# Attention with relative bias, then a bilinear feed-forward: fewer warm-up matmuls, another order around pairs 0, 1, 3 and 4, value products moved by one unit, and a last output tile stored in two halves

## The chip, the cores and the metric

The kernel runs on one core of a Trainium2 chip. The metric is the device time of one execution in microseconds (us). For the kernel before, the median of 11 runs is 427.14 us (425.99 to 428.47).

## The reference

The inputs are q, k and v in float32, each of 8 batches, 8 heads, 576 positions and 64 columns, a table of 32 bias buckets for 8 heads, and three weights: two of 512 x 1536 and one of 1536 x 512.

```python
scores = scale * np.matmul(q, k.transpose(0, 1, 3, 2))      # scale = 1/8
bias = bias_table[bucket]                                   # bucket depends on |i - j| alone
scores = scores + bias.transpose(2, 0, 1)[None, :, :, :]
attn = np.exp(scores - np.max(scores, axis=-1, keepdims=True))
attn = attn / (np.sum(attn, axis=-1, keepdims=True) + 1e-09)
x = np.matmul(attn, v).transpose(0, 2, 1, 3).reshape(8 * 576, 512)
out = ((x @ w_a) * (x @ w_b)) @ w_out                       # 4608 x 512, float32
```

## The kernel before, in words

**Pairs and steps.** The 64 combinations of batch and head are worked in 32 pairs of two heads; pair p belongs to batch p // 4. The 576 positions are four blocks of 128 and a tail of 64; the tails of the two heads share one block. For each pair TensorE (PE) makes the scores transposed, with keys on the partitions: `qk1(p, t)` (L334) for key block t, two matmuls of 64 x 512, one for each head, into one PSUM tile called `sc` of which there are two. `qk_tail(p)` (L361) makes the scores of the tails in a third use of the same two tiles and in a small extra bank. ScalarE (ACT) takes the exponential of each: `ex(p, t)` (L347) over 128 x 1024, `ex_tail(p)` (L374). VectorE (DVE) multiplies the band near the diagonal by exponentials of the bias: `mul` (L353) and `mul_tail` (L381), with tables `W` and `Wt` that a small matmul, an exponential and a trip through DRAM make at the start. `av(p, jq)` (L389) is the value product of query block jq, nine matmuls of 65 or 130 columns; blocks 0 to 2 go to one PSUM bank, 3 and 4 to another tile. A column of ones in the values gives the sums, and `norm(p, 0)` and `norm(p, 3)` (L441) divide by them on DVE and write `XG`. `t_x` (L456) transposes `XG` into the input `xn` of the feed-forward, either on PE (and then `c_x` copies it from PSUM) or, for the pairs in the set `XD` (L450), by DMA from the SP queue.

**q and k.** Both must be transposed before the scores. For pairs 0, 1 and 3 float32 inputs are transposed on PE (L559, L579, L588), for the other pairs of the first three batches bfloat16 inputs by `t_q` and `t_k` (L286, L306) with copies `c_q` and `c_k`; `tails_next` (L593) does the tails of the first pairs. From batch 3 on DMA transposes do this ("turns").

**The feed-forward.** Eight chunks of 512 positions, one for each batch, and a ninth chunk with all the tails. A chunk is 36 units of four matmuls of 128 x 128 x 512 each: 24 units `ff_a` and `ff_b` (L512, L518) for twelve slices of the hidden width, then four output tiles of three units, `ff_o` (L522). `ff_a` ends with a copy `ha` on ACT, `ff_b` with a product `g` on DVE, the third unit of an output tile with a copy `ob` on ACT and a store on the SP queue. The last chunk's stores are two for each tile, of 64 rows.

**PSUM.** Eight banks: four for the two `sc` tiles, one called AV, one called TR (transposes, and value products 3 and 4 of the early pairs), two called FF. From step 12 on (`R3`, L110) the units take turns on the two FF banks and TR, and value products 3 and 4 use AV, as do products 0 to 2.

**Order.** The order on each engine is that of the code. Pairs 0 to 2 are a loop (L601), pair 3 and the start of pair 4 are written out (L644 to L695), and from step 4 on a list of steps (L714 to L757) has places for units, marked U. A table of quotas says how many units a step puts there: 12, 7, 6, 4 and 4 in steps 4 to 8, nine in each later one. In step s pair s gets its scores and pair s-1 its value products. All loads of v, k, q and the weights but the first are issued by GpSimd (POOL) in one queue.

## Time and profile before

| | |
|---|---|
| median of 11 runs | 427.14 us (425.99 to 428.47) |
| profiled execution | 426.22 us |
| span from the first to the last instruction in it | 424.5 us |
| PE | busy 408.2 us, 96% of the span |
| ACT | busy 243.0 us, 57% |
| DVE | busy 199.0 us, 47% |
| POOL | busy 119.4 us, 28% |
| units' matmuls (lines L508 and L527) | 110.6, 109.6 and 99.5 us of PE's busy time |
| data moved | 40.31 MB |

The profiled execution takes 1.7 us more than its span, and lies 0.92 us under the median of the runs. A row of the time-ordered view gives the start, the duration, the engine, the line, what is written from what, and the count of merged instructions; in brackets stands how long the engine was idle before it and what ended that. A matmul's duration includes the time until its last result is out, so two neighbours overlap: of four matmuls of 512 columns in a row only the starts tell the pace. A few matmul records are missing. Some lines of the views name a releaser whose semaphore was in use again later, so the name is not always that of the true cause.

### The profile page before, as it was taken

How to read it: one execution, taken by the hardware profiler on the slowest of the kernel's cores; microseconds unless marked ns; L12 is line 12 of the kernel's file. 1: busy time of each engine (PE TensorE's matmuls, PEld its weight loads, DVE VectorE, ACT ScalarE, POOL GpSimd, SP SyncE). 2: the span in 40 equal slices, each digit the busy share in tenths (PEclk: the TensorE clock that was granted, in tenths of full speed). 3: DMA queues.
4: the chain of work that ended last, by engine and by line, in shares of the span. 5: the costliest groups of instructions: out<-in, count | busy, mean ns of one | idle time of the engine just before them, and what ended most of it. 6: DMA issues, size and time to landing. Idle time of an engine off the chain costs nothing.

```text
span 424.5 us, 8421 instructions
## 1 busy us (share of the span) xinstructions
PE 408.2 (96%) x3355; PEld 204.0 (48%) x3410; DVE 199.0 (47%) x492; ACT 243.0 (57%) x343; POOL 119.4 (28%) x161
## 2 busy tenths in 40 slices
PE   8798899999999999999999999999999999999995
PEld 3474455555544444444444444444444454444442
DVE  3684576556552555245535553355425550331420
ACT  3986476666665666676656665666656642322321
POOL 9998829603527000920073003000000000000000
PEclk9999999999999999999999999999999999999999
DMA  9999999993919950999099917931020012002004
GB/s 157 191 172 174 159 173 142 176 174 33 105 20 158 180 72 15 143 183 117 15 87 197 141 20 50 173 74 34 15 88 32 10 17 99 2 0 100 1 4 96
DMA packets 162855, 40.31 MB, mean 95 GB/s; under 512 B 153368, under 2 KB 158016, under 8 KB 162816
## 3 DMA queue, kind: packets, MB, share of 16 engines
q0 software_dynamic: 110448, 18.75, 60.4%
q1 hardware_dynamic: 51248, 20.72, 25.4%
q8 instruction: 26, 0.43, 0.4%
q10 hardware_dynamic: 1120, 0.30, 0.3%
q14 instruction: 13, 0.11, 0.1%
HBM read 38.77 MB, written 9.45 MB: 114 GB/s over the span
## 4 chain that ended last, share of the span: by engine, by line
PE 88%; POOL 4%; DMA 4%; issue 1%; DVE 1%; ACT 0%; POOLq 0%; DVEq 0%
PE pa L508 22%; PE pb L508 22%; PE po L527 22%; PE av L409 8%; PE qk L339 7%; PE av L400 3%; DMA vm<-in_v_dram 2%; DMA qtl<-in_q_dram 2%; PE qkt L364 2%; PE qkt L367 1%; DMA vt<-in_v_dram 1%; POOL vm L123 1%; PE trx L472 1%; POOL W L166 1%; PE trk L311 0%
## 5 line engine op out<-in xcount | busy, mean ns | idle before, releaser
L350 ACT ACTIVATE at<-qk 128x1024 bf16<-128x1024 f32 x128 | 126.0, 1024 | 21.9 <-PE qk L339 21.9
L520 DVE TENSOR_TENSOR g<-pb,ha 128x512 bf16<-128x512 f32 x108 | 74.7, 692 | 116.7 <-PE pb L508 95.1
L508 PE MATMUL pa<-xn,wa 128*128 128x512 bf16 x421 | 110.6, 379 | 2.3 <-ACT ha L515 1.6
L508 PE MATMUL pb<-xn,wb 128*128 128x512 bf16 x414 | 109.6, 379 | 0.8
L515 ACT ACTIVATE ha<-pa 128x512 f32<-128x512 f32 x108 | 64.6, 598 | 70.8 <-PE pa L508 69.3
L527 PE MATMUL po<-wo,g 128*128 128x512 bf16 x410 | 99.5, 379 | 1.2
L358 DVE TENSOR_TENSOR at<-at,W 128x512 bf16<-128x512 bf16 (+1 forms) x128 | 60.0, 483 | 9.8 <-ACT at L350 8.2
L508 PEld LDWEIGHTS <-wa 128*128 128x128 bf16 x432 | 38.9, 98 | 49.5 <-issue 10.3
L531 ACT ACTIVATE ob<-po 128x512 f32<-128x512 f32 x36 | 21.5, 597 | 69.9 <-PE po L527 67.9
L508 PEld LDWEIGHTS <-wb 128*128 128x128 bf16 x432 | 39.2, 98 | 45.5 <-issue 5.4
L527 PEld LDWEIGHTS <-g 128*128 128x128 bf16 x432 | 38.4, 98 | 45.4 <-issue 7.4
L123 POOL DMA_DIRECT2D vm<-in_v_dram x32 | 28.1, 906 | 106.6 <-PE av L409 105.4
L409 PE MATMUL av<-vm,at 128*128 128x65 bf16 x992 | 43.3, 193 | 0.0
L409 PEld LDWEIGHTS <-at 128*128 128x128 bf16 x992 | 39.5, 97 | 3.9
L445 DVE RECIPROCAL rc<-av 128x6 f32<-128x6 f32 x64 | 12.0, 188 | 57.2 <-PE av L409 55.4
L400 PE MATMUL av<-vt,att 128*128 128x130 bf16 x156 | 34.9, 224 | 0.4
L378 ACT ACTIVATE att<-qkt 128x1024 bf16<-128x1024 f32 x32 | 32.6, 1020 | 0.0
L446 DVE TENSOR_TENSOR XG<-av,rc 128x384 bf16<-128x384 f32 x64 | 31.4, 491 | 2.2
L123 POOL DMA_DIRECT2D qn<-in_q_dram x28 | 24.4, 926 | 26.7 <-PE trq L291 19.2
L123 POOL DMA_DIRECT2D kn<-in_k_dram x28 | 24.5, 920 | 5.6 <-DMA vm<-in_v_dram 2.5
L339 PE MATMUL qk<-QTb,KTb 64*128 64x512 bf16 x160 | 24.2, 381 | 0.0
L400 PEld LDWEIGHTS <-att 128*128 128x128 bf16 x156 | 15.3, 98 | 15.3 <-DVE XG L446 10.7
(114 smaller groups left out, 239.6 us busy)
## 6 DMA issues: line engine op xcount, KB each, us to landing
out_dram<-ob SPq DMA_DIRECT2D x32, 256.0 KB, 4.5
vm<-in_v_dram POOLq DMA_DIRECT2D x28, 128.0 KB, 5.2
qn<-in_q_dram POOLq DMA_DIRECT2D x24, 128.0 KB, 7.7
kn<-in_k_dram POOLq DMA_DIRECT2D x24, 128.0 KB, 8.9
wa<-in_moe_w_a_dram POOLq DMA_DIRECT2D x3, 512.0 KB, 7.0
wb<-in_moe_w_b_dram POOLq DMA_DIRECT2D x3, 512.0 KB, 8.8
wo<-in_moe_w_out_dram POOLq DMA_DIRECT2D x1, 1536.0 KB, 13.4
out_dram<-ob SPq DMA_DIRECT2D x8, 128.0 KB, 2.4
```

The source lines that it names most:

```text
L123: nc.gpsimd.dma_start(out=(vm[b % 2][:, h0:h1, t, 0:Dh] if dst is None else dst[b % 2][:, :].rearrange("p (t h d) -> p t h d", h=H, t=NM)[ ...
L339: nc.tensor.matmul(out=ps[:, hh, :], lhsT=kT_(p, t)[r, :], rhs=qT[r, :, :], start=True, stop=True)
L350: nc.scalar.activation(out=at[:, :, :], in_=ps[:, :, :], func=ACTF.Exp, scale=scale)
L358: nc.vector.tensor_tensor(out=at[:, :, lo:hi], in0=at[:, :, lo:hi], in1=w[:, :, y:(None if z < 0 else z):-1], op=MULT)
L378: nc.scalar.activation(out=at[:, 0:1024].rearrange("p (a x) -> p a x", a=2), in_=ps[:, :, :], func=ACTF.Exp, scale=scale)
L400: nc.tensor.matmul(out=pav[:, slot, :, :], lhsT=x, rhs=vt[b // 2 % 2][:, 4 * i + hp, :, 0:Dh + 1], start=fresh, stop=True, skip_group_chec ...
L409: nc.tensor.matmul(out=pav[:, slot, hh, :], lhsT=x, rhs=vm[i][:, 2 * hp + hh, t, 0:Dh + 1], start=False, stop=True, skip_group_check=True)
L446: nc.vector.tensor_tensor(out=xg[:, j0:j0 + n, :, :], in0=pav[:, 0:n, :, 0:Dh], in1=rc.unsqueeze(3).to_broadcast([128, n, 2, Dh]), op=MULT)
L508: nc.tensor.matmul(out=ff[key][:, :], lhsT=w[df // FW][:, mc, 128 * (df % FW):128 * (df % FW) + 128], rhs=xn_sb[mc][:, xin(c)], start=(i = ...
L515: nc.scalar.activation(out=ha[:, :], in_=ff["pa"][:, :], func=ACTF.Copy)
L520: nc.vector.tensor_tensor(out=g_sb[df][:, :], in0=ff["pb"][:, :], in1=ff["ha"][:, :], op=MULT)
L527: nc.tensor.matmul(out=po[:, :], lhsT=g_sb[df][:, 128 * tt:128 * tt + 128], rhs=wo_sb[:, df, :], start=(df == 0), stop=(df == NDF - 1))
```

## The change

It has six parts.

1. Five warm-up matmuls on zeros ahead of the first transposes become three. Two such matmuls are put elsewhere: one ahead of the second and one ahead of the third score block of pair 0 (`fill`).
2. The first turn of the loop over pairs 0 to 2 is written out. In it the first score block of pair 1 and its exponential stand ahead of the tail scores of pair 0, and the multiplications `mul(0, 0)` to `mul(0, 2)` behind them.
3. At pair 3 the copy `c_x(2)` goes from DVE to ACT, the transposes `t_k(4)` stand behind the value products of pair 3, and all scores of pair 4 move behind the first units, into step 4, whose list now has a unit at each of twelve places and ends with two of them.
4. In steps 5 to 10 `t_k(s + 1)` stands one place for a unit later, behind `mul(s, 2)`.
5. From step 12 on, value products 3 and 4, `norm(s-1, 3)` and the DMA transposes behind them come one unit later. The set `XD` begins at pair 8 instead of pair 11, so that pairs 8, 9 and 10 are transposed by DMA.
6. The last output tile of the last chunk is made in two halves of 256 columns, in two PSUM banks. The first half is copied on ACT, the second on DVE, and of each half 64 rows are stored from the SP queue and 64 from ACT's.

The change moves instructions. On ACT, at pairs 0 and 1 (`at0_3` is pair 0's fourth exponential, `att0` takes that of the tails), the kernel before has

```order
L350 ACTIVATE at0_2_314<-qk0_2_294 128x1024
L350 ACTIVATE at0_3_334<-qk0_3_311 128x1024
L377 ACTIVATE att0_94<-qktt0_329 128x64
L378 ACTIVATE att0_94<-qkt0_323 128x1024
L350 ACTIVATE at1_0_345<-qk1_0_336 128x1024
L350 ACTIVATE at1_1_359<-qk1_1_342 128x1024
```

and the changed kernel has, in the same place,

```order
L353 ACTIVATE at0_2_314<-qk0_2_293 128x1024
L353 ACTIVATE at0_3_326<-qk0_3_311 128x1024
L353 ACTIVATE at1_0_328<-qk1_0_323 128x1024
L380 ACTIVATE att0_94<-qktt0_336 128x64
L381 ACTIVATE att0_94<-qkt0_330 128x1024
L353 ACTIVATE at1_1_359<-qk1_1_344 128x1024
```

One exponential of pair 1 has moved ahead of the two of pair 0's tails.

On ACT, between pair 3 and the first units (`trx2` is `c_x(2)`, `trq4` and `trk4` are the transposes of pair 4, `ha0_0` is the copy of the first unit), the kernel before has

```order
L350 ACTIVATE at3_3_662<-qk3_3_658 128x1024
L255 ACTIVATE QT0_121<-trq4_686 128x512
L255 ACTIVATE KT0_123<-trk4_691 128x512
L350 ACTIVATE at4_0_742<-qk4_0_739 128x1024
L350 ACTIVATE at4_1_753<-qk4_1_744 128x1024
L350 ACTIVATE at4_2_770<-qk4_2_767 128x1024
L350 ACTIVATE at4_3_777<-qk4_3_774 128x1024
L515 ACTIVATE ha0_0_780<-pa0_0_747 128x512
L515 ACTIVATE ha0_1_794<-pa0_1_789 128x512
```

and the changed kernel

```order
L353 ACTIVATE at3_3_662<-qk3_3_658 128x1024
L255 ACTIVATE xn2_138<-trx2_664 128x512
L255 ACTIVATE xn2_138<-trx2_664 128x64
L255 ACTIVATE QT0_121<-trq4_686 128x512
L255 ACTIVATE KT0_123<-trk4_733 128x512
L518 ACTIVATE ha0_0_760<-pa0_0_743 128x512
L353 ACTIVATE at4_0_767<-qk4_0_764 128x1024
L518 ACTIVATE ha0_1_777<-pa0_1_772 128x512
L353 ACTIVATE at4_1_779<-qk4_1_769 128x1024
L353 ACTIVATE at4_2_790<-qk4_2_781 128x1024
L353 ACTIVATE at4_3_795<-qk4_3_792 128x1024
```

The copies of the first two units have moved from behind all four exponentials of pair 4 to places ahead of the first and the second of them, and the copy of pair 2's transposes has come in.

On DVE, in a late step (`rc21` with `av21_0` and `av21_3` are the two norms of pair 21, `at22` the multiplications of pair 22, `g` the products of units), the kernel before has

```order
L445 RECIPROCAL rc21_3495<-av21_0_3496 128x6
L446 TENSOR_TENSOR XG1_126<-av21_0_3496,rc21_3495 128x384
L520 TENSOR_TENSOR g3_143<-pb4_3_3526,ha4_3_3491 128x512
L358 TENSOR_TENSOR at22_0_3484<-at22_0_3484,W2_91 128x2x256
L445 RECIPROCAL rc21_3495<-av21_3_3533 128x4
L446 TENSOR_TENSOR XG1_126<-av21_3_3533,rc21_3495 128x256
L358 TENSOR_TENSOR at22_1_3493<-at22_1_3493,W2_91 128x2x384
```

and the changed kernel

```order
L448 RECIPROCAL rc21_3477<-av21_0_3478 128x6
L449 TENSOR_TENSOR XG1_126<-av21_0_3478,rc21_3477 128x384
L523 TENSOR_TENSOR g3_143<-pb4_3_3508,ha4_3_3473 128x512
L361 TENSOR_TENSOR at22_0_3466<-at22_0_3466,W2_91 128x2x256
L361 TENSOR_TENSOR at22_1_3475<-at22_1_3475,W2_91 128x2x384
L448 RECIPROCAL rc21_3477<-av21_3_3523 128x4
L449 TENSOR_TENSOR XG1_126<-av21_3_3523,rc21_3477 128x256
```

The second norm has moved behind the next multiplication, since the value products that it reads come a unit later.

The diff, cut to its core:

```diff
-    warm_up(5)
+    warm_up(3)
...
-    def qk1(p, t):
+    def qk1(p, t, fill=0):
...
+        for _ in range(fill):
+            nc.tensor.matmul(out=ps[:, 0, :], lhsT=zero_sb[:, 0:128], rhs=zero_sb[:, :],
+                             start=True, stop=True)
...
-    XD = set(range(11, NP - 1))
+    XD = set(range(8, NP - 1))
...
+    def ff_last(c, tt):
+        ob = obp.tile([128, DM], FP32, tag="ob", name=f"ob{c}_{tt}")
+        for x, cols in enumerate((slice(0, 256), slice(256, 512))):
+            po = ff_bank(f"po{c}_{tt}_{x}")
+            for df in range(NDF):
+                nc.tensor.matmul(out=po[:, cols], lhsT=g_sb[df][:, 128 * tt:128 * tt + 128],
+                                 rhs=wo_sb[:, df, cols], start=(df == 0), stop=(df == NDF - 1))
+            copy(None if x else nc.scalar, ob[:, cols], po[:, cols])
+            for hh, eng in enumerate((nc.sync, nc.scalar)):
+                r0 = S * (2 * tt + hh) + SM
+                eng.dma_start(out=out[r0:r0 + ST, cols], in_=ob[64 * hh:64 * hh + 64, cols])
...
+    qk1(0, 3)
+    ex(0, 2)
+    tails_next(0, 2, None)
+    qk1(1, 0)
+    ex(0, 3)
+    ex(1, 0)
+    qk_tail(0)
+    mul(0, 0)
+    mul(0, 1)
+    ex_tail(0)
+    mul(0, 2)
+    qk1(1, 1)
...
-    c_x(2)
+    c_x(2, ACT)
     t_q(4, FF)
-    t_k(4, FF)
     c_q(4, ACT)
-    c_k(4, ACT)
...
-    qk1(4, 0)
-    ex(4, 0)
-    qk1(4, 1)
+    t_k(4, FF)
+    c_k(4, ACT)
+    norm(3, 0)
+    norm(3, 3)
     ff_mm(0, 0, wa_sb, "pa", 0, 3)
...
         if s == 4:
...
+            steps += [U, U, lambda: qk1(4, 0), lambda: ex(4, 0), lambda: qk1(4, 1), U, lambda: ex(4, 1),
+                      lambda: qk1(4, 2), U, lambda: ex(4, 2), lambda: qk1(4, 3), lambda: ex(4, 3),
+                      lambda: mul(4, 0), U, tails4, U, lambda: qk_tail(4), lambda: ex_tail(4),
+                      lambda: mul(4, 1), U, lambda: mul(4, 2), U, lambda: mul(4, 3),
+                      lambda: mul_tail(4), U, lambda: t_q(5, TR), lambda: c_q(5), U,
+                      lambda: t_k(5, TR), lambda: c_k(5), U, U]
...
+            av34 = [A(3, 4), N(3)]
             if s - 1 in XD:
-                steps += [lambda: t_x(s - 1), lambda: turns(s)]
...
+                av34 += [lambda: t_x(s - 1), lambda: turns(s)]
+            if s < R3:
+                steps += av34
+            steps += [U, lambda: mul(s, 1)]
+            if s >= R3:
+                steps += av34
+            steps += [lambda: qk(s, 2), lambda: ex(s, 2)]
...
-            steps += [U, lambda: ex(s, 3)]
+            steps += [U, lambda: ex(s, 3), U, lambda: mul(s, 2)]
             if e:
                 steps += [lambda: t_k(s + 1, TR), lambda: c_k(s + 1)]
-            steps += [U, lambda: mul(s, 2), U, lambda: mul(s, 3),
-                      lambda: qk_tail(s), lambda: ex_tail(s), U]
+            steps += [U, lambda: mul(s, 3), lambda: qk_tail(s), lambda: ex_tail(s), U]
```

More of the change, by code (lines that the diff above doesn't have):

```diff
@@ L540, with last @@
     units = []
+    def last(part):
+        if part == 0:
+            ff_last(NCH - 1, 3)
     for c in range(NCH):
@@ L547 @@
             for part in range(3):
-                units.append(lambda c=c, tt=tt, part=part: ff_o(c, tt, part))
+                if c == NCH - 1 and tt == 3:
+                    units.append(lambda part=part: last(part))
+                else:
+                    units.append(lambda c=c, tt=tt, part=part: ff_o(c, tt, part))
     nxt = 0
@@ L609 @@
         k_next(s)
[L610 to L614 removed]
         qk1(s, 3)
         ex(s, 2)
[L617 to L620 removed]
+        tails_next(s + 1, 1, ACT)
         qk_tail(s)
         mul(s, 0)
[L623 to L627 removed]
+        av(s - 1, 0)
+        av(s - 1, 1)
+        av(s - 1, 2)
+        norm(s - 1, 0)
         mul(s, 1)
         ex(s, 3)
[L630 to L631 removed]
+        av(s - 1, 3, FF)
         qk1(s + 1, 0)
         ex_tail(s)
[L634 to L636 removed]
+        av(s - 1, 4)
+        norm(s - 1, 3)
         mul(s, 2)
```

55 lines of the change are left out of this document (17 added, 38 removed).

## The prediction, as it was put on record before the changed kernel ran

> **What bounds the kernel now.** I read the page first, for the share of each engine and the slices over time, then the table of waits for PE, then the time-ordered rows around each wait. From the page:
>
> ```profile
> PE 408.2 (96%) x3355; PEld 204.0 (48%) x3410; DVE 199.0 (47%) x492; ACT 243.0 (57%) x343; POOL 119.4 (28%) x161
> PE   8798899999999999999999999999999999999995
> PEclk9999999999999999999999999999999999999999
> DMA  9999999993919950999099917931020012002004
> ```
>
> PE is busy in nine tenths or more of nearly every slice of 10.6 us; only four of the first five slices and the last have less. So time can be won only where PE stands still (at the start, at the end, or in stalls too short for this digit), or by taking matmuls away. The waits of PE, and of its weight loads, as the tables give them:
>
> ```profile
> PE pa L508 <- ACT ha L515: 1.6, 1, 1.6
> PE qk L339 <- DVE KT L257: 1.3, 2, 1.0
> PEld L400 <- DVE XG L446: 10.7, 21, 0.5
> ```
>
> The first two are three waits in the first 50 us. The third comes 21 times: a weight load of the value products waits for a norm on DVE, once in each step from 12 to 32. What it costs PE itself has to be read from the starts of the matmuls.
>
> **The late steps (20 times one stall).** The rows of one late step:
>
> ```profile
> 215.35 2.76 PE L527 MATMUL po<-wo,g 128*128 128x512 bf16 x12
> ...
> 223.45 1.03 PE L527 MATMUL po<-wo,g 128*128 128x512 bf16 x4
> 224.50 0.23 PE L400 MATMUL av<-vt,att 128*128 128x130 bf16 x1
> ...
> 223.89 0.56 DVE L446 TENSOR_TENSOR XG<-av,rc 128x384 bf16<-128x384 f32 x1
> ```
>
> The first row gives the pace: twelve matmuls in 2.76 us, of which the last takes 0.38 to its end, so (2.76 - 0.38) / 11 = 0.216 each. The unit that starts at 223.45 therefore leaves PE free at 223.45 + 4 x 0.216 = 224.31. The next value product starts at 224.50, just after `XG` is written at 224.45: products 3 and 4 use the bank that the norm of products 0 to 2 is still reading. PE loses 0.18 to 0.19 us; I take 0.18. With one more unit ahead, 0.86 us, the norm is over 0.68 us before the bank is wanted. Steps 12 to 31 change, step 32 does not: 20 x 0.18 = **3.6 us**. What moves behind it, the second norm and a DMA transpose, is wanted no sooner than the next step, so I cost it at nothing; if a bank or a copy behind it is late instead, up to 0.05 us a step comes back. Bounds 2.6 to 3.8.
>
> **Three transposes less.**
>
> ```profile
> 94.51 0.44 PE L472 MATMUL trx<-cst_sb,XG 128*128 128x128 bf16 x5
> 94.78 0.38 PE L508 MATMUL pa<-xn,wa 128*128 128x512 bf16 x1
> ```
>
> The five transposes of a pair hold PE for 94.78 - 94.51 = 0.27 us. Pairs 8, 9 and 10 lose them: 3 x 0.27 = **0.8 us**. Their place is taken by six DMA transposes in SP's queue, ahead of a turn and of output stores. The chunk that reads them starts after step 12, a step or more later, and a store that waits holds only one of four `ob` buffers; that cover gone, a late store would stop ACT's copies. Bounds 0.5 to 0.9.
>
> **`t_k` one place later.**
>
> ```profile
> 80.86 0.40 PE L291 MATMUL trq<-cst_sb,qn 128*128 128x128 bf16 x4
> 81.77 0.38 PE L311 MATMUL trk<-cst_sb,kn 128*128 128x128 bf16 x4 [0.52 <-DVE QT L257]
> 82.05 0.22 PE L303 MATMUL trk<-cst_sb,qtl 128*128 128x128 bf16 x1
> ...
> 82.31 0.56 DVE L257 COPY KT<-trk 128x768 bf16<-128x768 bf16 x1 [0.58 <-PE trk L303]
> ```
>
> Step 8 puts no unit between `t_q` and `t_k`, which share the bank TR. Four transposes take (82.05 - 81.77) / 5 = 0.056 each, so PE could go on at 80.86 + 0.22 = 81.08; it goes on at 81.77, 0.68 late, after the copy on DVE. Step 7 has the same stall (next fence). In the new order a unit stands between them, and the stall goes. But now, with quotas 6, 4 and 4, no unit stands between `t_k` and `qk_tail` in steps 6, 7 and 8, whose last two matmuls want TR again: the copy of `KT` ends 82.87 - 82.05 = 0.82 after the last transpose starts, and only 4 x 0.056 + 0.216 = 0.44 us of tail matmuls (four of 128 columns, one of 512) lie between. So about 0.35 us is lost three times: 2 x 0.68 - 3 x 0.35 = **0.3 us** won. Bounds -0.5 (a loss) to 1.3.
>
> The unit also moves `t_k(8)` past a load that is just in time:
>
> ```profile
> 73.52 0.38 PE L311 MATMUL trk<-cst_sb,kn 128*128 128x128 bf16 x4 [0.52 <-DMA vt<-in_v_dram]
> ...
> 62.79 3.52 POOL L123 DMA_DIRECT2D kn<-in_k_dram  x4
> ...
> kn<-in_k_dram POOLq DMA_DIRECT2D x2, 128.0 KB, 5.0
> ```
>
> The last of the four loads of k is issued at about 65.4 (62.79 + 3.52 - 0.92) and lands 5.0 us later, near 70.4. Without its stall PE would have come here at 72.84; by the sums below it comes 2.4 us earlier and one unit later in its order, at 72.84 - 2.4 + 0.86 = 71.3. The load is in time, but a lead of over 3.3 us at this point would be given back to it.
>
> **The start: pairs 0 to 2.**
>
> ```profile
> 4.40 2.31 PE L212 MATMUL warm<-zero_sb 128*128 128x512 bf16 x5
> 6.50 0.42 PE L559 MATMUL trk0a<-id,k 128*128 128x128 f32 x1
> ...
> 11.40 0.30 PE L596 MATMUL trt<-id,kt 128*128 128x128 f32 x1 [0.22 <-DMA kt<-in_k_dram]
> 11.77 0.27 PE L596 MATMUL trt<-id,qt 128*128 128x128 f32 x1
> 12.56 0.40 PE L364 MATMUL qkt<-KT 128*128 128x128 bf16 x4 [0.52 <-DVE KT L257]
> ...
> 8.73 3.77 ACT L350 ACTIVATE at<-qk 128x1024 bf16<-128x1024 f32 x4 [0.96 <-PE qk L339]
> 13.27 0.22 ACT L377 ACTIVATE att<-qktt 128x64 bf16<-128x64 f32 x1 [0.77 <-PE qktt L370]
> 14.29 2.87 ACT L350 ACTIVATE at<-qk 128x1024 bf16<-128x1024 f32 x3
> ...
> 14.40:28.40 14.00, 13.20 (x203) 9.40 (x205) 11.55 (x35) 13.45 (x20) 13.02 (x22) 1.00 1.50 181
> ```
>
> The last row is a stretch of 14 us with the busy time of PE, weight loads, DVE, ACT and POOL: ACT is busy for 13.45 of it. From 8.73 on it does exponentials nearly without a break, 0.94 each (3.77 / 4), so here ACT sets the pace, and its one real gap is the 0.77 us ahead of 13.27. There it waits for the tails' scores, which wait for copies, which wait for transposes that start at 11.40 when the tails of k land. None of this moves. What moves is one score block of pair 1: right behind the four transposes, whose last starts at 11.77, so at 11.9, and its exponential from 0.4 later (12.33) to 13.27. The tails' exponential starts at 13.27 as before, with one exponential more behind it: 0.94 us. A little is lost again, since pair 1's tail scores now meet the copies that queue behind the first multiplications on DVE: I take **0.85 us**. Two warm-ups less let the transposes start up to 2 x (6.50 - 4.40) / 5 = 0.84 us sooner (the row of 6.50 shows no wait, so the loads had landed; how much sooner isn't shown: 0 to 0.84). But ACT then only waits longer ahead of 12.33: of the 0.84, 8.73 + 3.77 - 12.33 = 0.17 us at most is needed, and is in the sum. The two fills lie where PE waits, for a copy and for ACT. Bounds 0.3 to 1.2.
>
> A rule of the Trainium skill bears on the warm-ups. A matmul of 512 columns takes 0.42 us before 6.5 us and 0.216 at 215 us, while the row of granted clocks on the page of the profile shows nine tenths or more throughout: PE starts at half pace. "TensorE: Matmul & The Clock Gate", Part 1, says that the clock opens after a busy stretch of some 3.4 us, in windows that run free of the kernel, and not after a number of matmuls; by that, two fewer cost nothing as long as PE stays busy. What would be otherwise is the third rival.
>
> **Pairs 3 and 4.**
>
> ```profile
> 29.94 0.52 DVE L257 COPY xn<-trx 128x512 bf16<-128x512 bf16 x2
> 30.60 0.38 PE L311 MATMUL trk<-cst_sb,kn 128*128 128x128 bf16 x4 [0.29 <-DMA qtl<-in_q_dram]
> ...
> 34.83 1.94 ACT L350 ACTIVATE at<-qk 128x1024 bf16<-128x1024 f32 x2 [0.28 <-PE qk L339]
> 37.31 1.02 PE L508 MATMUL pa<-xn,wa 128*128 128x512 bf16 x4 [1.63 <-ACT ha L515]
> 48.44 0.61 PE L339 MATMUL qk<-QT,KT 64*128 64x512 bf16 x4 [0.99 <-DVE KT L257]
> ```
>
> Three stalls. At 30.60 `t_k(4)` waits 0.29, not for the load named but for its bank, which the copy of pair 2 releases at 30.46. At 37.31 the second unit waits 1.63: its bank is freed by the first unit's copy `ha`, which stands on ACT behind exponentials until 36.77. At 48.44 pair 5's scores wait 0.99 for the copy of `KT`. Together 2.9 us. The new order removes all three: the copy is on ACT and `t_k(4)` later, the first `ha` stands ahead of the exponentials, and two units cover the last copy. It makes new ones: pair 4's scores no longer fill the time in which pair 3's norms run, about 0.5 us between the two groups of transposes, and the fourth score block waits for the second exponential, which now stands behind a second `ha`, about 0.5 us (an exponential of 0.97 and a copy of 0.6, as the one of the same size at 419.60 below, against a unit of 0.86 and a score block of 0.3). 2.9 - 1.0 = **1.9 us**. Bounds 0.7 to 2.9.
>
> **The end.**
>
> ```profile
> 419.60 0.60 ACT L531 ACTIVATE ob<-po 128x512 f32<-128x512 f32 x1 [1.99 <-PE po L527]
> 420.22 1.10 SPq L538 DMA_DIRECT2D out_dram<-ob  x2
> ...
> DMA to landing us min/median/max: 2.3/2.4/2.5
> ...
> 7.81 0.42 DVE L257 CAST QT<-trq0b 128x256 bf16<-128x256 f32 x1 [0.56 <-PE trq0b L559]
> ```
>
> Last comes a copy of 0.60, then two stores issued one behind the other, the second 0.52 after the first, and 2.4 to its landing. After the change the last copy is 256 columns on DVE, 0.42 by the nearest row, and the two stores are issued at once from two queues: 0.18 + 0.52 = **0.7 us**. PE makes 24 matmuls of half the columns in the same 2.6 us. Bounds 0.2 (ACT's queue is slower) to 0.9 (smaller stores land sooner).
>
> **Sum.** 3.6 + 0.8 + 0.3 + 0.85 + 1.9 + 0.7 = 8.15 us. The profiled execution of 426.22 would become 418.1; it lies 0.92 under the median of the runs, so against the median 427.14 - 8.15 = **419.0 us**. The bounds add up to 3.8 and 11.0, but hardly all lie on one side: 417.4 to 420.6 is the forecast's own range.
>
> **Rivals.**
>
> *The start doesn't pay.* In the first nine slices, 95 us, the page's row has DMA busy all the time, and what PE wins in the first 50 us it may lose again waiting for weights, values or k. For it: the load above, 0.5 us from being late. Against it: 37.31 and 48.44 wait for ACT and DVE, not for loads. Then 0.85 + 1.9 + 0.3 go: 427.14 - 5.1 = 422.0. Chance 0.12.
>
> *The late stall moves.* Products 3 and 4 come later and something behind them waits instead: 427.14 - (8.15 - 3.6) = 422.6. Against it: 0.68 us to spare. Chance 0.05.
>
> *The clock opens a window late*, since fewer warm-ups leave gaps before 8 us. Were PE at half pace until 11.40, the eight transposes of pair 1, about 0.12 each by the rows from 11.40 to 11.77, would take twice that, and three score blocks and two fills 0.2 more each: about 2 us, of which more than half is hidden by waits. ACT would stall near 0.9, and the result be 419.9. For it, by the rule named above: the windows are not tied to the start. Chance 0.07.
>
> *Slower.* In each late step two units now stand back to back, each wanting one of three banks that ACT or DVE must free, with exponentials in ACT's queue. In step 4, with two banks, such neighbours cost PE this:
>
> ```profile
> 40.39 1.03 PE L508 MATMUL pb<-xn,wb 128*128 128x512 bf16 x4
> 41.41 1.02 PE L508 MATMUL pa<-xn,wa 128*128 128x512 bf16 x4
> ```
>
> 1.02 from start to start instead of 0.86, so 0.16. At 0.15 a step 3 us come back: 422.0. At 0.41 a step (8.15 / 20) the gain is gone; at 0.5 it would be 429.0. Against it: those were two banks, and these are three; the twelve matmuls at 215.35 are three units back to back, at full pace. Chance 0.06, half of it at the point of no change and half beyond.
>
> The forecast has 0.70. The range takes in the rivals up to 422 and the forecast's lower end: 416.8 to 422.1. What a measurement of this kernel can tell from no change is about 0.2%, 0.9 us: faster 0.94, same 0.03, slower 0.03.
>
> **What would show it.** In the profile after: the wait of those weight loads for `XG` once instead of 21 times, and 0.18 us less from step to step; no wait for `ha` near 35 us and none for `KT` ahead of pair 5, whose scores start near 45.7 instead of 48.44; ACT's gap ahead of 13.27 halved; 4.2 us instead of 4.9 from the start of the last copy to the end of the span. I am wrong if the late steps keep their length, or if pair 5's scores start early and pair 8's wait for k by as much.

## The result, and the profile after

The changed kernel takes 418.41 us, the median of 8 runs (418.01 to 418.92); the kernel before 427.15 us (31 runs, 425.89 to 428.62). The ratio is 0.979, with a 95% interval of 0.978 to 0.981: 8.7 us less. The profiled execution took 418.21 us with a span of 416.4, against 426.22 and 424.5: 8.0 and 8.1 less.

The page of the changed kernel, with busy times and the slices of PE and of the DMA engines:

```profile
PE 404.6 (97%) x3350; PEld 208.0 (50%) x3407; DVE 197.5 (47%) x485; ACT 245.5 (59%) x345; POOL 119.4 (29%) x161
PE   8899999999999999999999999999999999999996
DMA  9999999999929950999099908921120102002004
```

PE is busy for 3.6 us less, and idle for 416.4 - 404.6 = 11.8 us instead of 16.3. Which term is which has to be read from waits and starts. The table of waits of the changed kernel (engine, what waits, on what; us in all, times, longest):

```profile
PEld L403 <- DVE XG L449: 0.5, 1, 0.5
PE qktt L373 <- DVE KT L257: 1.0, 4, 0.4
```

The wait for `XG` is there once, in step 32, instead of 21 times, and the waits for `ha` and for `KT` ahead of a pair's scores are gone. The second row is new: the last two matmuls of the tails' scores wait for the copy of `KT`.

**The late steps.** One step of the changed kernel, in order of time:

```profile
218.64 1.89 PE L542 MATMUL po<-wo,g 128*128 128x512 bf16 x7
219.07 0.56 DVE L449 TENSOR_TENSOR XG<-av,rc 128x384 bf16<-128x384 f32 x1
220.37 0.22 PE L403 MATMUL av<-vt,att 128*128 128x130 bf16 x1
```

Two units stand here (one of eight records is missing) and last 220.37 - 218.64 = 1.73 us, which is 8 x 0.216: no wait between them, and none behind. `XG` is written at 219.63, 0.74 before product 3 wants its bank.

**The start.** Pairs 0 and 1 on PE and ACT:

```profile
5.70 0.45 PE L581 MATMUL trk0a<-id,k 128*128 128x128 f32 x1
5.94 0.64 PE L581 MATMUL trq0a<-id,q 128*128 128x128 f32 x2
8.22 5.26 ACT L353 ACTIVATE at<-qk 128x1024 bf16<-128x1024 f32 x5 [1.23 <-PE qk L342]
9.20 0.66 PE L581 MATMUL trq<-id,q 128*128 128x128 f32 x4
11.45 0.30 PE L618 MATMUL trt<-id,kt 128*128 128x128 f32 x1
13.38 0.22 ACT L380 ACTIVATE att<-qktt 128x64 bf16<-128x64 f32 x1
```

Five exponentials run without a break from 8.22 to 13.48, and the tails' follow at 13.38 with no gap named; before, four ran and then ACT waited 0.77 us.

**Pairs 3 to 5.** The places of the three old stalls:

```profile
31.69 0.34 PE L475 MATMUL trx<-cst_sb,XG 128*128 128x128 bf16 x3
32.24 0.28 PE L475 MATMUL trx<-cst_sb,XG 128*128 128x128 bf16 x2 [0.21 <-DVE XG L449]
33.45 0.60 ACT L518 ACTIVATE ha<-pa 128x512 f32<-128x512 f32 x1 [1.73 <-PE pa L511]
35.40 1.04 PE L511 MATMUL pb<-xn,wb 128*128 128x512 bf16 x4
36.74 0.39 PE L342 MATMUL qk<-QT,KT 64*128 64x512 bf16 x2 [0.31 <-ACT at L353]
45.40 0.60 PE L342 MATMUL qk<-QT,KT 64*128 64x512 bf16 x4
```

The first copy `ha` runs at 33.45 behind its unit. The two new stalls stand where they were foreseen, ahead of the second group of transposes and of the fourth score block. The brackets say 0.21 and 0.31, but a bracket counts from the end of the last matmul. By the starts PE loses 32.24 - (31.69 + 3 x 0.056) = 0.38 and 36.74 - (35.40 + 4 x 0.216) = 0.48, together 0.86. Pair 5's scores start at 45.40 instead of 48.44.

The old stalls are larger by their starts too. These rows of the kernel before stand ahead of the three stalls that the prediction shows:

```profile
29.92 0.38 PE L291 MATMUL trq<-cst_sb,qn 128*128 128x128 bf16 x4
35.46 0.22 PE L303 MATMUL trt<-cst_sb,qtl 128*128 128x128 bf16 x1
47.24 0.22 PE L303 MATMUL trk<-cst_sb,qtl 128*128 128x128 bf16 x1
```

At 0.056 for each transpose PE could go on at 30.14, 35.52 and 47.30; it goes on at 30.60, 37.31 and 48.44, so it loses 0.46, 1.79 and 1.14, together 3.39 us, where the brackets give 2.9.

**`t_k` in its new place.** Steps 5, 6 and 7:

```profile
52.65 0.55 DVE L361 TENSOR_TENSOR at<-at,W 128x768 bf16<-128x768 bf16 x1
53.12 0.55 DVE L257 COPY KT<-trk 128x768 bf16<-128x768 bf16 x1
53.72 0.22 PE L373 MATMUL qktt<-KT 128*128 128x64 bf16 x2 [0.36 <-DVE KT L257]
...
63.07 0.38 PE L370 MATMUL qkt<-QT,KT 128*128 128x512 bf16 x1
63.66 0.22 PE L373 MATMUL qktt<-KT 128*128 128x64 bf16 x2 [0.21 <-DVE KT L257]
...
63.66 3.52 POOL L123 DMA_DIRECT2D kn<-in_k_dram  x4
...
71.33 0.39 PE L311 MATMUL trk<-cst_sb,kn 128*128 128x128 bf16 x4
```

In step 6 the last matmuls start at 63.66 instead of 63.07 + 0.216 = 63.29, so 0.37 us is lost, and the same in steps 7 and 8. Steps 5 and 9 lose 0.31 each (53.72 instead of 52.97 + 0.44, the pace of the five matmuls ahead, and 90.91 instead of 90.16 + 0.44). `t_k(8)` starts at 71.33 and waits for nothing: its load had landed. But the four loads of that k start to be issued at 63.66, against 62.79 in the kernel before, although PE is 3 us ahead here: they don't move with PE. In both kernels, and in four of the experiments below, they start 14.5 to 15.4 us after the issue of the output weights in the same queue (48.66 here, 48.01 before).

**The end.** The last output tile:

```profile
409.87 2.78 PE L530 MATMUL po<-wo,g 128*128 128x256 bf16 x24
411.38 0.38 ACT L255 ACTIVATE ob<-po 128x256 f32<-128x256 f32 x1 [0.71 <-PE po L530]
411.79 1.85 ACTq L535 DMA_DIRECT2D out_dram<-ob  x2
411.90 1.71 SPq L535 DMA_DIRECT2D out_dram<-ob  x2
412.69 0.42 DVE L257 COPY ob<-po 128x256 f32<-128x256 f32 x1 [9.63 <-PE po L530]
```

From the start of the last copy, 412.69, to the end of the span there are 3.7 us, against 4.9 before.

**Where the time went.** A marker that all the kernels share is the first matmul of each pair's tail scores. The table has its start in the changed kernel's profiled execution, and for every other kernel how much later (+) or sooner (-) it starts there. The last column is the span.

| us | pair 1 | pair 5 | pair 10 | pair 12 | pair 31 | span |
|---|---|---|---|---|---|---|
| changed kernel | 16.40 | 52.97 | 102.23 | 124.65 | 334.83 | 416.4 |
| kernel before | +0.81 | +3.05 | +2.82 | +3.27 | +6.94 | +8.1 |
| changed kernel, again | -0.18 | -0.19 | -0.19 | -0.19 | -0.20 | -0.2 |
| late steps undone | -0.04 | +0.17 | +0.18 | +0.37 | +4.03 | +4.1 |
| `XD` from pair 11 | -0.30 | -0.20 | +0.10 | +0.36 | +0.36 | +0.6 |
| `t_k` at its old place | +0.22 | +0.22 | +0.69 | +0.69 | +0.68 | +0.7 |
| pairs 0 to 2 undone | +0.72 | +0.72 | +0.73 | +0.73 | +0.72 | +0.8 |
| five warm-ups | -0.20 | +0.12 | +0.12 | +0.12 | +0.11 | +0.2 |
| no warm-ups | +0.59 | +0.60 | +0.60 | +0.60 | +0.60 | +0.6 |
| pairs 3 and 4 undone | +0.02 | +2.25 | +2.42 | +2.42 | +2.41 | +2.5 |
| last tile whole | +0.20 | +0.19 | +0.19 | +0.20 | +0.19 | +0.9 |
| units placed by hand | -0.22 | +0.31 | -0.85 | -0.85 | -0.85 | -1.0 |
| the same, again | -0.11 | +0.15 | -0.91 | -0.90 | -0.91 | -1.1 |
| the same, `t_k(8)` later | -0.10 | +0.61 | -0.34 | -0.33 | -0.34 | -0.5 |

The changed kernel's second execution is 0.2 away from its first from the first pairs on, so a constant shift of that size says nothing. A shift that arises between two pairs says something only where the code between them differs. Between pairs 1 and 2 some executions shift by 0.2 to 0.7 us though their code there is the changed kernel's: 0.71 in the last row, where PE waits 0.68 for a load of k ahead of 20.97, and 0.53 in the row of the units placed by hand. So each effect below is read between pairs where the code differs. From pair 12 to 31 a step lasts (334.83 - 124.65) / 19 = 11.062 us, against 11.255 before.

### The profile page after: what moved, and what is told of

It is laid out like the page before. It is cut to its first block, busy times and chain, and to the rows that moved or that the text cites. A ratio compares the mean times of both kernels' runs of the same rounds, so it can differ in the third digit from the quotient of the medians.

```text
span 416.4 us, 8424 instructions
## 1 busy us (share of the span) xinstructions
PE 404.6 (97%) x3350; PEld 208.0 (50%) x3407; DVE 197.5 (47%) x485; ACT 245.5 (59%) x345; POOL 119.4 (29%) x161
## 4 chain that ended last, share of the span: by engine, by line
PE 91%; DVE 3%; DMA 2%; ACT 1%; issue 1%; SPq 0%; ACTq 0%; DVEq 0%
PE pb L511 22%; PE pa L511 22%; PE po L542 22%; PE av L412 9%; PE qk L342 8%; PE av L403 2%; PE qkt L367 1%; PE qkt L370 1%; DMA kt<-in_k_dram 1%; ACT at L353 1%; DMA k<-in_k_dram 1%; PE qktt L373 1%; PE trx L475 1%; PE po L530 1%; DVE KT L257 1%
## 5 line engine op out<-in xcount | busy, mean ns | idle before, releaser
L542 PE MATMUL po<-wo,g 128*128 128x512 bf16 x403 | 96.3, 379 | 1.1 <-issue 0.3
L361 DVE TENSOR_TENSOR at<-at,W 128x512 bf16<-128x512 bf16 (+1 forms) x128 | 59.1, 484 | 6.9 <-ACT at L353 5.5
```

Source lines behind the costliest of these rows:

```text
L361: nc.vector.tensor_tensor(out=at[:, :, lo:hi], in0=at[:, :, lo:hi], in1=w[:, :, y:(None if z < 0 else z):-1], op=MULT)
L542: nc.tensor.matmul(out=po[:, :], lhsT=g_sb[df][:, 128 * tt:128 * tt + 128], rhs=wo_sb[:, df, :], start=(df == 0), stop=(df == NDF - 1))
```

## The experiments

Each undoes or alters one part of the changed kernel.

**The late steps undone.** Value products 3 and 4 stand in their early place in all steps.

```diff
-            if s < R3:
-                steps += av34
+            steps += av34
             steps += [U, lambda: mul(s, 1)]
-            if s >= R3:
-                steps += av34
```

> The changed kernel, but value products 3 and 4, the second norm and the DMA transposes behind them stand at their early place in all steps, one unit sooner than in the changed kernel from step 12 on. Theory (a stall of 0.18 us on PE in each of steps 12 to 31, because the products wait for the norm that reads their bank): the weight load of the value products waits for XG 21 times again, a late step takes 11.26 us instead of 11.06, the span is 3.6 to 3.9 us longer than the changed kernel's 416.4, about 420.2, and the median near 422.2 against 418.4. Rival (the wait of the weight load is idle time that PE hides anyway, and the late steps got shorter by something else): span and median within 0.5 us of the changed kernel.

It takes 422.82 us (422.23 to 424.48; ratio to before 0.990, 0.987 to 0.993). In its table of waits

```profile
PEld L403 <- DVE XG L449: 10.7, 21, 0.5
```

is back, and from pair 11 to pair 31 it falls 4.03 - 0.18 = 3.85 us behind, 0.193 in each of 20 steps. Nothing of the gain was given back: the stall went, and no other came.

**`t_k` at its old place.**

```diff
-            steps += [U, lambda: ex(s, 3), U, lambda: mul(s, 2)]
+            steps += [U, lambda: ex(s, 3)]
             if e:
                 steps += [lambda: t_k(s + 1, TR), lambda: c_k(s + 1)]
-            steps += [U, lambda: mul(s, 3), lambda: qk_tail(s), lambda: ex_tail(s), U]
+            steps += [U, lambda: mul(s, 2), U, lambda: mul(s, 3), lambda: qk_tail(s), lambda: ex_tail(s), U]
```

> The changed kernel, but t_k(s + 1) and its copy stand at their old place, ahead of the unit and of mul(s, 2). Theory from the two traces: the later place is a small loss. The stall between t_q and t_k of steps 7 and 8 (0.68 each, 1.36 together) comes back, and the stall of the last tail scores behind the copy of KT (0.31, 0.37, 0.37, 0.37 and 0.31 in steps 5 to 9, 1.73 together) goes: the span 0.4 us shorter than 416.4, about 416.0. Rival (the sum of the prediction, in which steps 5 and 9 lose nothing): the later place wins 0.3 us, so the span here is 416.7.

It takes 419.15 us (418.42 to 420.24). It loses 0.69 - 0.22 = 0.47 between pairs 5 and 10. The expectation's theory had a gain of 0.4; its rival, the prediction's sum, had a loss of 0.3, but not for the cause found here. Its rows in step 7 say why:

```profile
70.69 0.33 PE L311 MATMUL trk<-cst_sb,kn 128*128 128x128 bf16 x3 [0.52 <-DVE QT L257]
71.68 0.23 PE L311 MATMUL trk<-cst_sb,kn 128*128 128x128 bf16 x1 [0.66 <-DMA kn<-in_k_dram]
```

The old stall of 0.68 for the bank is back ahead of 70.69, as expected, and once more a step later. But then the fourth transpose waits for the last load of k: by the pace it would start at 70.69 + 3 x 0.056 = 70.86 and it starts at 71.68, 0.82 late. With the five new stalls gone (3 x 0.37 + 2 x 0.31 = 1.73), the two old ones back (1.36) and this one (0.82), the sum is 0.45 lost; 0.47 was measured. So, beside the kernel before, moving `t_k` costs 0.37 us; in the changed kernel, whose PE comes here 3 us sooner, it still pays, because a `t_k` in the old place would wait for its load.

**Pairs 3 and 4 undone.** The order from pair 3 to step 4 is that of the kernel before.

```diff
-    c_x(2, ACT)
+    c_x(2)
...
+    t_k(4, FF)
...
+    qk1(4, 0)
+    ex(4, 0)
+    qk1(4, 1)
+    ff_mm(0, 0, wa_sb, "pa", 0, 3)
...
-            steps += [U, U, lambda: qk1(4, 0), lambda: ex(4, 0), lambda: qk1(4, 1), U, lambda: ex(4, 1),
...
+            steps += [U, tails4, lambda: mul(4, 0), U, lambda: qk_tail(4), lambda: ex_tail(4), lambda: mul(4, 1), U, lambda: mul(4, 2),
...
```

> The changed kernel, but pair 3's end, pair 4's scores and the list of step 4 are as in the kernel before: pair 2's copy on DVE, t_k(4) early, all four exponentials of pair 4 ahead of the first unit's copy, no units at the end of step 4. Theory: PE's three waits come back (for the bank at t_k(4), for ha at the second unit, for KT ahead of pair 5's scores), pair 5's scores start 2.2 us later than the changed kernel's 45.4, near 47.6, and all of it stays to the end: span about 418.6, median about 420.6. Rival (loads set the pace until 95 us, so a later start of pair 5 is caught up by step 12, since units wait less): pair 5 later by 2.2 us, the span longer by less than 1 us.

It takes 420.95 us (420.66 to 421.30; ratio 0.985, 0.982 to 0.988). PE's three waits are back:

```profile
29.80 0.38 PE L311 MATMUL trk<-cst_sb,kn 128*128 128x128 bf16 x4 [0.29 <-DVE xn L257]
36.51 1.02 PE L511 MATMUL pa<-xn,wa 128*128 128x512 bf16 x4 [1.62 <-ACT ha L518]
47.65 0.60 PE L342 MATMUL qk<-QT,KT 64*128 64x512 bf16 x4 [0.99 <-DVE KT L257]
```

and 2.25 us are lost by pair 5, 2.4 from pair 10 to the end. The rival, that later loads take the gain back, falls.

**Pairs 0 to 2 undone**, with three warm-ups and two fills kept: the loop of the kernel before.

```diff
-    qk1(1, 0)
-    ex(0, 3)
-    ex(1, 0)
-    qk_tail(0)
...
+    for s in range(3):
+        ex(s, 0)
...
+        qk1(s, 2, 1 if s == 0 else 0)
```

> The changed kernel, but pair 0's tail scores and their exponential stand ahead of pair 1's first score block again, with the shorter warm-up and the two fills kept. Theory (the tails of k land at a fixed time, and what was won is one exponential of ACT behind that wait): ACT idles about 1.3 us ahead of pair 0's tails, 0.5 more than in the kernel before since its first exponential starts sooner, pair 2's first scores start 0.8 us later than the changed kernel's, and the span is 0.8 us longer, 417.2. Rival (the first exponentials start sooner by 0.5 us thanks to the warm-ups, and that is the gain): span within 0.3 us of 416.4.

It takes 419.12 us (418.94 to 420.35) and is 0.72 us behind from pair 1 to the end. Pair 0's tail scores stand 0.14 sooner than in the changed kernel (12.47 against 12.61), so 0.86 arises between pairs 0 and 1. ACT's gap is back, and longer than in the kernel before (0.77), since the exponentials began sooner:

```profile
13.18 0.22 ACT L380 ACTIVATE att<-qktt 128x64 bf16<-128x64 f32 x1 [1.17 <-PE qktt L373]
```

**Five warm-ups, no fills.**

```diff
-    warm_up(3)
+    warm_up(5)
...
-    qk1(0, 1, 1)
+    qk1(0, 1)
...
-    qk1(0, 2, 1)
+    qk1(0, 2)
```

> The changed kernel with five warm-up matmuls ahead of the first transposes again and without the two fills. Theory: the first exponential starts 0.5 to 0.6 us later, near 8.75, but ACT has a wait ahead of pair 1's first exponential to lose, so pair 1's tail scores are 0.2 us later than the changed kernel's 16.4 at the most, and the span is 416.4 to 416.7. Rival (the warm-ups are on the path): span 0.8 us longer, 417.2. The clock's opening, seen in the pace of the matmuls, is expected between 7.5 and 10 us as in all of these profiles, whatever the number of warm-ups.

It takes 418.67 us (418.27 to 421.05), no difference that can be told. The rows of its start:

```profile
5.99 0.27 PE L581 MATMUL trk0a<-id,k 128*128 128x128 f32 x1
6.10 0.38 PE L581 MATMUL trq0a<-id,q 128*128 128x128 f32 x2
...
11.25 0.30 PE L618 MATMUL trt<-id,kt 128*128 128x128 f32 x1 [1.22 <-DMA kt<-in_k_dram]
12.26 1.02 ACT L353 ACTIVATE at<-qk 128x1024 bf16<-128x1024 f32 x1 [0.84 <-PE qk L342]
```

In this execution PE was at full pace early, not from 7.5 to 10 us on as was expected: 6.10 - 5.99 = 0.11 us for a transpose, where the changed kernel shows 5.94 - 5.70 = 0.24. The scores came sooner, and then PE waited 1.22 for the tails of k and ACT 0.84 for pair 1's block behind them. A faster start is worth nothing past this load.

**No warm-ups** behind the matmul for the table.

```diff
-    warm_up(3)
+    warm_up(0)
```

> The changed kernel with no warm-up matmul between the table's matmul and the first transposes; the fills and the five first warm-ups stay. Theory: PE now waits for the loads of q and k, which land at 5.6 to 5.7, so the transposes start no sooner than the changed kernel's 5.70 and nothing is won; PE idles about 1.1 us. If the clock opens by how long PE was busy, it opens a window later, after 10 us, and pair 1's scores and transposes run at half pace until then: pair 0's tail scores stay bound to their load at 11.4 and the span is 416.4 to 417.4. Rival (the loads have landed sooner, warm-ups only hold PE): the transposes start near 4.5 to 5 us, and the span is unchanged or shorter by up to 0.3 us.

It takes 418.84 us (418.71 to 419.13), 0.4 more than the changed kernel in the median with ranges that overlap, and its profiled execution is 0.60 behind from pair 1 on:

```profile
5.89 0.45 PE L581 MATMUL trk0a<-id,k 128*128 128x128 f32 x1 [1.43 <-DMA k<-in_k_dram]
...
9.38 1.12 PE L581 MATMUL trq<-id,q 128*128 128x128 f32 x4
...
11.22 1.94 ACT L353 ACTIVATE at<-qk 128x1024 bf16<-128x1024 f32 x2 [0.71 <-PE qk L342]
```

PE waits for the first k until 5.89, so fewer warm-ups than three, with which it starts at 5.70, win nothing there. And PE is slow for longer: four transposes take 1.12 at 9.38, against 0.66 in the changed kernel's row at 9.20, which made ACT wait 0.71. This is the stall that the prediction's rival of a late clock put at 0.9; here it was 0.6. One profiled execution doesn't show that the missing warm-ups made the pace late: with three of them it began before 8.12 in one execution and after 8.65 in another.

**`XD` from pair 11**, so that PE transposes pairs 8 to 10 again.

```diff
-    XD = set(range(8, NP - 1))
+    XD = set(range(11, NP - 1))
```

> The changed kernel with the DMA transposes of the feed-forward's input from pair 11 on instead of pair 8. Theory: the five transposes of pairs 8, 9 and 10 hold PE for 0.27 us each again: 0.8 us between the tail scores of pairs 8 and 12, and the span 0.8 us longer. Rival (DMA transposes cost something elsewhere in these steps): less than 0.5 us. The start of pair 2 may differ between runs by a few tenths and is subtracted.

One execution: 418.77 us. Against the changed kernel the tail scores of pairs 8, 10, 11 and 12 stand at -0.20, +0.10, +0.23 and +0.36, so the three pairs cost 0.30, 0.13 and 0.13, 0.56 in all, not 0.8. The rows of the end of step 10 here, where pair 9 is transposed:

```profile
103.69 0.44 PE L475 MATMUL trx<-cst_sb,XG 128*128 128x128 bf16 x5
103.97 1.03 PE L511 MATMUL pb<-xn,wb 128*128 128x512 bf16 x4
104.83 1.03 PE L511 MATMUL pa<-xn,wa 128*128 128x512 bf16 x4
```

and in the changed kernel:

```profile
103.59 1.03 PE L511 MATMUL pb<-xn,wb 128*128 128x512 bf16 x4
103.95 0.60 ACT L518 ACTIVATE ha<-pa 128x512 f32<-128x512 f32 x1
104.61 1.02 PE L511 MATMUL pa<-xn,wa 128*128 128x512 bf16 x4
```

With the transposes, 0.28 us, the second unit follows the first after 0.86. Without them it follows after 1.02. The views name no releaser for it, but by the program the units take turns on two banks, and this one's is freed by the copy `ha`, which ends at 104.55, 0.06 ahead of the unit; so 0.16 of the 0.28 becomes a wait. In steps 9 and 11 the same 0.15 is lost at this place, there behind the product `g`: it ends at 92.79 and 115.77, and the units start at 92.84 and 115.82.

Pair 8 is worth 0.30 all the same, since with `XD` from 11 the transposes of q in step 10 start 0.70 after the score block ahead of them instead of 0.54 (in the kernel before it was 0.54 too). Their bank, TR, is read by pair 9's second norm, which ends at 99.11 here (98.82 in the changed kernel), 0.06 ahead of them. The norm is late behind a product `g` that starts at 97.54 instead of 97.25; what that one waits for stays open.

**The last tile whole**, as in the kernel before.

```diff
-                if c == NCH - 1 and tt == 3:
-                    units.append(lambda part=part: last(part))
-                else:
-                    units.append(lambda c=c, tt=tt, part=part: ff_o(c, tt, part))
+                units.append(lambda c=c, tt=tt, part=part: ff_o(c, tt, part))
```

> The changed kernel with the last output tile made and stored whole, as in the kernel before. Theory: the last copy is again 0.60 us on ACT and the two stores go out one behind the other, so the end of the span lies 4.86 us behind the start of the last copy as in the kernel before, against 3.75 in the changed kernel, while PE gets its twelve wide matmuls in 0.03 us less: 1.1 us from the last matmul to the end, of which the prediction had 0.7. Rival (0.7, and the rest of the 1.1 is chance in the landing of two stores): 4.4 us behind the start of the last copy.

One execution: 419.11 us. Its last copy:

```profile
412.85 0.60 ACT L546 ACTIVATE ob<-po 128x512 f32<-128x512 f32 x1 [1.99 <-PE po L542]
```

From the start of that copy to the end of the span (417.3) there are 4.45 us. The same work took 4.9 in the kernel before, so 0.4 of the difference between the profiled executions is scatter of what follows the last stores. The halves are worth 0.9 - 0.19 = 0.7 us here, the predicted size. From the table, span less the mark of pair 31, the stretch to the end is 81.6 to 81.8 us in the nine executions with halves and the same step 32, 82.3 in this one and 82.7 in the kernel before: a gain in any case, of 0.5 to 1.2 us.

**Units placed by hand.** If the cause of the stalls in steps 5 to 9 is the place of the units, then `t_k` in its old place with a unit on both sides has neither. So `t_k` goes back, steps 6 to 9 get their units from a list, and in step 32 products 3 and 4 come one unit later too.

```diff
-    quotas = {4: 12, 5: 7, 6: 6, 7: 4, 8: 4}
+    quotas = {4: 12, 5: 7, 6: 6, 7: 5, 8: 5, 9: 7}
+    places = {6: (1, 0, 1, 1, 1, 0, 1, 1, 0), 7: (1, 0, 1, 1, 1, 0, 1, 0, 0), 8: (1, 0, 1, 1, 1, 0, 1, 0, 0),
+              9: (1, 1, 1, 1, 1, 1, 1, 0, 0)}
...
-            steps += [U, lambda: ex(s, 3), U, lambda: mul(s, 2)]
+            steps += [U, lambda: ex(s, 3)]
...
-            steps += [A(0, 1, 2), N(0), U, A(3, 4), N(3), U, lambda: t_x(s - 1, AV),
+            steps += [A(0, 1, 2), N(0), U, U, A(3, 4), N(3), U, lambda: t_x(s - 1, AV),
...
-                n = (quota * seen + nu - 1) // nu - put
+                n = places[s][seen - 1] if s in places else (quota * seen + nu - 1) // nu - put
```

> The changed kernel with t_k(s + 1) at its old place, but with the units of steps 6 to 9 put where they cover the bank TR: one between value products 4 and t_q, one between t_q and t_k, and one between t_k and the tail scores (quotas 6, 5, 5, 7 in steps 6 to 9 instead of 6, 4, 4, 9). In step 32 products 3 and 4 come one unit later too. Theory (the bank TR is what stalls PE in steps 5 to 9): the stalls of 0.31, 0.37, 0.37, 0.37 and 0.31 behind the copy of KT, that of 0.35 ahead of t_q in step 6 and that of 0.18 in step 32 go, 2.2 us together, less what the new places cost: span 414.3 to 415, median near 416.5. Rival (loads set the pace there, and PE then waits for k, v or the output weights instead): span within 0.5 us of 416.4, with waits of PE for DMA between 50 and 90 us.

It takes 416.77 us (416.44 to 417.17; ratio 0.976, 0.973 to 0.979). It wins 0.31 + 0.85 = 1.16 us between pairs 5 and 10. To compare it closely, the changed kernel and this one ran again on one chip:

> The changed kernel once more, beside the next one. Median 418.4 as before, within 0.5. The span of the profiled execution varies with the last load of k for pair 3, which landed between 18.8 and 20.8 us in the profiles so far and is wanted at 20.15: 416.4 if it is in time, up to 0.8 longer if not.

> The kernel with the units placed around the bank TR once more, beside the changed kernel, on the same chip. Theory (its stalls in steps 5 to 9 and 32 are gone but for the wait for the last load of k, 0.5 to 0.8 us at 70.8): 1.2 to 1.7 us faster than the changed kernel in the median. Rival (the first run was a lucky landing of loads): less than 0.5 us between the two.

The changed kernel took 418.46 (four runs, 418.13 to 418.82; ratio 0.980, 0.979 to 0.982), this one 417.15 (five runs, 417.06 to 418.00; ratio 0.978, 0.976 to 0.980). The ranges don't meet, and the medians are 1.3 us apart, the spans 0.9. It is faster than both kernels. In step 7 it still loses time:

```profile
70.53 0.33 PE L311 MATMUL trk<-cst_sb,kn 128*128 128x128 bf16 x3
71.48 0.23 PE L311 MATMUL trk<-cst_sb,kn 128*128 128x128 bf16 x1 [0.61 <-DMA kn<-in_k_dram]
```

The table of waits names no wait of PE for a bank between 45 and 127 us any more, but the last load of k is 71.48 - (70.53 + 0.17) = 0.78 us late.

**The same, with `t_k(8)` a unit later**, behind the load.

```diff
-              ... 7: (1, 0, 1, 1, 1, 0, 1, 0, 0), 8: ...
+              ... 7: (1, 0, 1, 1, 1, 1, 0, 0, 0), 8: ...
...
+            tk = [lambda: t_k(s + 1, TR), lambda: c_k(s + 1)] if e else []
+            steps += [U] + tk if s == 7 else tk + [U]
```

> The kernel with the units placed around the bank TR (span 415.4), but in step 7 t_k(8) comes one unit later, with a unit on each side of it. Theory (in that kernel t_k(8) waits 0.66 us at 70.8 for the last load of k, which lands at about 71.4): the wait goes, PE does a unit in that time, and the span is 0.6 to 0.7 us shorter, 414.7 to 414.8, median near 416.1. Rival (the next load behind it, or the copy of KT, is late instead): span within 0.2 us of 415.4.

It takes 417.61 us (416.94 to 418.85). The wait for the load is gone, but the unit is now missing in another place, where

```profile
74.11 0.44 PE L475 MATMUL trx<-cst_sb,XG 128*128 128x128 bf16 x5 [0.31 <-ACT att L380]
```

and a score block behind it wait. From pair 5 to pair 10 it wins 0.61 + 0.34 = 0.95, against 1.16 and 1.06 with `t_k(8)` ahead of the load. So the load is not what holds this stretch alone; it looks as if there were too few units for all the places that want one, but no run tests that.

## Why the prediction was right or wrong, point by point

The sum was 8.15 us; the medians are 8.7 apart, the profiled executions 8.0 and the spans 8.1, and 418.4 lies 0.6 from the 419.0 forecast. These 0.6 are not in the sum: the forecast let the changed kernel's median lie 0.92 above its profiled execution, as before the change, and it lies 0.20 above. That the sum came so close is partly luck. Two terms were too large, together by 1.1 us, and three others too small, together by 1.0. By the table, for the two profiled executions:

| term | predicted | from the two traces | undone alone |
|---|---|---|---|
| late steps | 3.6 | 3.86 (20 x 0.193) | 3.85 |
| three transposes less | 0.8 | 0.39 | 0.56 |
| `t_k` later | 0.3 | -0.37 | 0.47 |
| pairs 0 to 2 | 0.85 | 0.81 | 0.72 |
| pairs 3 and 4 | 1.9 | 3.05 - 0.81 = 2.24 | 2.25 to 2.4 |
| end | 0.7 | 1.1 | 0.7 |
| sum | 8.15 | 8.0 | 8.5 to 8.7 |

- *Late steps:* right. The step was 0.18, at the low end of what the rows gave (0.18 to 0.19); it measured 0.193. The cost of what moves behind, taken as nothing, is nothing. The slower rival, units back to back that wait for their banks, doesn't show in these steps: 1.73 us for two units.
- *Three transposes less:* the step that failed is "3 x 0.27". PE's time for them was right (0.28), but the place left empty was not asked about: in each of the three steps the next unit came to its bank about 0.15 too early. That is the rival's mechanism, with the price of its row (1.02 for a unit instead of 0.86), in steps 9 to 11 with two banks. "From the two traces" is 3 x 0.13: the 0.28 less that wait, in each of the three pairs.
- *`t_k` later:* wrong in sign beside the kernel before. The two old stalls went and the three foreseen ones came (0.37 for 0.35). What failed is that only steps 6, 7 and 8 were counted. In step 5 and step 9 a unit does stand between `t_k` and the tails' scores, but the copy of `KT` stands on DVE behind a multiplication that ends at 53.20, and comes 0.31 too late all the same. The order on DVE had to be read too, not only on PE. The marks agree: from pair 5 to pair 10 the lead shrinks by 3.05 - 2.82 = 0.23, which is 0.37 less the 0.13 that pair 8's transposes are worth. The load of k behaved as the warning had it: it had landed when the changed kernel wanted its last part, at 71.33 + 3 x 0.056 = 71.50, and two other executions, which wanted it 0.6 to 0.8 us sooner (70.86 and 70.70), waited for it until 71.68 and 71.48.
- *Pairs 0 to 2:* right. One exponential of pair 1 fills ACT's gap. The gap is gone and not halved, as the prediction had it: the exponentials begin at 8.22 instead of 8.73 and five of them take 5.26, so they last up to the tails' scores.
- *Warm-ups and fills:* right that two warm-ups less cost nothing and win nothing: five of them without fills gave no difference that can be told. With none, the profiled execution lost 0.6. The third rival, full pace that begins late, is real in that execution, and cheaper than put: 0.6 for 0.9. The rule of the Trainium skill named in the prediction ("TensorE: Matmul & The Clock Gate", Part 1: windows of about 3.4 us that run free of the kernel, no count of matmuls) agrees with the traces in that the number of matmuls doesn't decide: with the same five warm-ups the first transpose lasts 0.27 us at 5.99 in one kernel, and 0.42 at 6.50 in the kernel before (a row of the prediction). The length of its windows doesn't account for the time: in the changed kernel no wait of PE is named from 1.20 us to 12.61, yet the score block that starts at 8.65 takes 0.61, as at half pace, against 0.39 from 10.00 on; that is 7.4 us after PE's first matmul, over twice 3.4. The traces don't show why.
- *Pairs 3 and 4:* right in mechanism. The term was too small since its old stalls were read from the brackets, 2.9, where the starts give 3.39; the new ones, 0.86 by the starts, were sized nearly right (1.0). Of the 2.5 which that leaves, 2.24 was measured; what takes the rest stays open. All three old stalls came back when the part was undone, and nothing later took the gain back, so the first rival falls.
- *End:* right by its own price in the one execution that undoes it. Of the 1.1 against the kernel before, 0.4 comes after the last copy has started, between two executions of the same work.

What stays open: what holds the product `g` at 97.54 with `XD` from 11, when and why PE comes to full pace, and why the same last stores are followed by 4.45 us in one execution and 4.9 in another.

## What to carry to other kernels

When a step moves or matmuls go, look at what they covered: on PE the next matmul's bank, on DVE and ACT the copies queued ahead of the one that frees it. A move can be worth nothing or less beside the old kernel and still be needed in the new one, because a lead won earlier runs into a load that doesn't move with it; so undo parts alone from the new kernel as well as adding up differences from the old. Size a stall from the starts and the pace of the matmuls ahead of it, not from the bracket: here three brackets left out about 0.16 us each. Where units of filler work are short, a list of places for each step did better here than an even spread.

## What the runs showed of the hardware that wasn't expected

- PE comes to full pace at a time that changes from one execution to the next: before 5.99 us with five warm-ups in one kernel, after 6.50 with the same five in the kernel before, with three before 8.12 in one kernel (pairs 0 to 2 undone, where a fill lasts 0.39) and after 8.65 in the changed one (where the fill at 8.12 lasts 0.61), and after 9.38 with none. The row of granted clocks on the page shows nine tenths or more from its first slice in the changed kernel too, so the pace must be read from like matmuls (0.24 and 0.11 us from start to start for a float32 transpose of 128 columns).
- While the DMA engines are busy all the time, a load need not move with PE. PE reached pair 7 three microseconds sooner than before the change, but the loads of k for pair 8 were issued from 63.66 on, against 62.79 before.
- The landing of one load scatters by a microsecond between executions: the k that PE transposes for pair 3 was there at 19.96 with `XD` from 11, and was waited for until 20.97 in the last experiment, with the same code up to there.
